# Token scaling ahead of the last weight maxima, and transfers of the token squares one step behind their data

## The chip, the cores and the metric

The kernel runs on 1 core of one Trainium2 chip. The metric is the device time of one execution in microseconds (us): the median of repeated runs of the whole kernel.

## The reference

A gated convolution over the sequence feeds a two-layer network:

```python
w = exp(weight_gen - max(weight_gen, -1)); w = w / (sum(w, -1) + 1e-09)      # 7 taps, 8 heads
out = einsum('bshk,bskhg->bshg', w, x_unf)      # x_unf: the 7 last rows of x, heads of 24
h = out.reshape(16384, 192) @ w_in              # w_in: 192 x 2048
g = maximum(0.01 * h, h)
return g @ w_out                                # w_out: 2048 x 192
```

All inputs and the output are float32.

## The kernel before, in words

The 16384 tokens are worked on in 32 chunks of 512 (`NCH`, `TOK`), and the 2048 hidden columns in 8 pairs of blocks of 128 (`NQ`). One call of `step(q)` (line 722) does pair i = q % 8 of chunk c = q // 8, so that step 8 is the first of chunk 1 and step 16 the first of chunk 2. In a step, `mm1` (line 495) forms the hidden values `hp` of two blocks in PSUM, ScalarE applies the leak and copies a float16 upper half `gh`, VectorE subtracts to get the lower half `gl` (`split_g`, line 525), and `mm2_pass` (line 548) multiplies halves of the step before with `wo` into the sums `po`. The second product is cut in two: `mm2_first` does two rows of the sums, then `tell` (line 570) puts an empty instruction on SyncE's queue that waits for its last matmul, and the first matmul of `mm2_second`, in the next step behind that step's `mm1`, waits for that empty instruction. SyncE's queue runs in order, so whatever stands ahead of a tell there holds it up. `hp` has four PSUM buffers, so that `mm1` of a step needs the buffers that `split_g` of the step but one before has read.

From chunk 1 on, both products run on pairs of float16 numbers: a token or weight is scaled by a power of two and split in an upper and a lower half. For the weights this needs the maxima over all blocks (`most`, line 186), joined by `weight_scales(0)`, `(1)` and `(2)` (line 212) across TensorE and VectorE into `scale`; `upper_half` (ScalarE) and `lower_half` (VectorE) then write `wi_h`, `wi_l` and `wo` block by block. Chunk 0 runs in float32 (`mm2_whole`, line 593, for its second product).

The tokens of chunk c + 1 go through a chain while chunk c is multiplied:

- GpSimd forms them by 13 operations of `conv_ops` (line 334), handed out by `feed`;
- `scale_tokens` (line 438): VectorE takes the maximum `xm`, computes the powers `xu` and `xd`, GpSimd multiplies (line 450);
- `split_h` (ScalarE, line 454) and `split_l` (GpSimd, line 463) make the halves; `split_h` also has VectorE compute `xr`, by which the sums are scaled back in `evacuate`;
- `squares` (line 467): four transposes of 32 x 32 blocks on VectorE;
- `put_squares` (line 478): SyncE sends them to DRAM (`far<-sq`), 384 KB;
- `get_squares` (line 485): SyncE waits for that and fetches them back in four transfers (`xx<-far`), 192 KB each, 32 partitions each. The first two feed the first half of the partitions of `mm1`, the last two the second half.

In `step`, `scale_tokens` comes in step i = `first`, the halves in `first + 1`, squares and `put_squares` in `first + 2`, `get_squares` in `first + 3`; `first` is 1, but 3 in chunk 1 and 2 in chunk 2 (`BEGIN`, line 43).

Everything before step 8 is ordered by hand in the string `START` (line 53): one letter for each action, in program order of all engines. The letters that matter here: `f` is `mm1` of the next pair of chunk 0 with its leaks, `e` the second product of one block of chunk 0, `m` the maximum of one weight block, `W` its rounding, `D` the division in the softmax of piece 1, `B` is `scale_tokens(1)`, `C` `split_h(1)`, `V` `split_l(1)`, `y` and `Y` the transposes of its two halves, `X` `put_squares(1)`, `R` `get_squares(1)`, `1 2 3` are the weight scales, `H` and `L` an upper and a lower half of a weight block, `q` one operation of chunk 2's convolution.

Of the kernel before, what the change touches and what calls it, by code (L numbers as in the profile page):

```python
# [8 lines left out]
F32 = mybir.dt.float32  # L9
F32R = mybir.dt.float32r  # L10
U32 = mybir.dt.uint32
I32 = mybir.dt.int32
F16 = mybir.dt.float16
AF = mybir.ActivationFunctionType
ALU = mybir.AluOpType
# [3 lines left out]
P = 128  # L19
# [20 lines left out]

HOLD = 2

BEGIN = {1: 3, 2: 2}

G0 = 20

# [9 lines left out]
    "rWrWmpf"  # L56
    "rWmrWmmKppeeeerWmprWmkppf"
    "rWmrWmMppf"
    "rWmrWmEpWmDpeeeef"
    "mmmmf"  # L60
    "B1e2e3CVyHLe"
    "HYLXe"
    "qRHLf"
    "qHLe"
    "qHLe"
)


# [1 line left out]
def conv_attention_moe_kernel(  # L70
# [8 lines left out]
    nc = tc.nc  # L79
# [8 lines left out]
    J = 4  # L88
# [16 lines left out]
    win = ctx.enter_context(tc.tile_pool(name="win", bufs=2))  # L105
# [77 lines left out]
    undo = const.tile([P, 1], F32, name="undo")  # L183
# [9 lines left out]
    def exponents(m, e):  # L193

        nc.vector.tensor_scalar(
            out=e, in0=m.bitcast(I32), scalar1=EXPONENT, scalar2=None, op0=ALU.bitwise_and
        )

    def powers(e, up, down):

        nc.vector.tensor_scalar(
            out=down, in0=e, scalar1=float(LEAST), scalar2=float(TOP * ONE),
            op0=ALU.max, op1=ALU.subtract,
        )
        nc.vector.tensor_scalar(  # L205
            out=up, in0=down, scalar1=-1.0, scalar2=float(254 * ONE),
            op0=ALU.mult, op1=ALU.add,
        )
# [56 lines left out]
    def load_weights(q, s=slice(0, R)):  # L265
        r0 = piece[q] * R
        if q not in wt:
            wt[q] = win.tile([P, R, HK], F32, tag="wt", name="wt")
        nc.sync.dma_start(out=wt[q][:, s, :], in_=w_rows[:, r0 + s.start:r0 + s.stop, :])

    def load_rows(q, parts=((0, PAD + R),)):
        r0 = piece[q] * R
        if q not in xt:
            xt[q] = xin.tile([P, PAD + R, D], F32, tag="xt", name="xt")
        if r0 > 0:
            for a, b in parts:
                nc.sync.dma_start(out=xt[q][:, a:b, :], in_=x_rows[:, r0 - PAD + a:r0 - PAD + b, :])
            return
        nc.sync.dma_start(out=xt[q][:, PAD:, :], in_=x_rows[:, 0:R, :])
        nc.gpsimd.memset(xt[q][0:1, 0:PAD, :], 0.0)  # L280
        for a, b in ((16, P), (1, 16)):
            nc.sync.dma_start(
                out=xt[q][a:b, 0:PAD, :], in_=x_rows[a - 1:b - 1, ROWS - PAD:ROWS, :]
            )
        for b in range(1, B):
            nc.gpsimd.memset(xt[q][b * PB:b * PB + 1, 0:PAD, :], 0.0)
# [9 lines left out]
    def softmax_max(q, s=ALL):  # L296
        if q not in mx:
            mx[q] = win.tile([P, R * H, 1], F32, tag="mx", name="mx")
            sm[q] = win.tile([P, R * H, 1], F32, tag="sm", name="sm")
        m = mx[q][:, s.start * H:s.stop * H, :]  # L300
        return nc.vector.tensor_reduce(out=m, in_=grouped(q, s), axis=AX.X, op=ALU.max).ins

    def softmax_sub(q, eng, s=ALL):
        eng.tensor_tensor(
            out=grouped(q, s), in0=grouped(q, s), in1=spread(mx[q], s), op=ALU.subtract
        )
# [86 lines left out]
    def new_xx(c):  # L393
        if c < WHOLE:
            xx[c] = xtp.tile([P, NK, 1, NB, P], F32, tag="xw", name="xw")
        else:
            xx[c] = xtp.tile([P, NK, 2, NB, P], F16, tag="xx", name="xx", bufs=2)
# [38 lines left out]
    split, sq, undo_of, downs = {}, {}, {}, {}  # L436

    def scale_tokens(c):

        m = win.tile([P, J, 2], F32, tag="xm", name="xm")[:, :, 0]  # L440
        e = win.tile([P, J, 2], I32, tag="xe", name="xe")[:, :, 0]
        up = win.tile([P, J, 2], I32, tag="xu", name="xu")[:, :, 0:1]
        down = win.tile([P, J, 2], I32, tag="xd", name="xd")[:, :, 0]
        nc.vector.tensor_reduce(  # L444
            out=m, in_=att[c], axis=AX.X, op=ALU.max, apply_absolute_value=True
        )
        exponents(m, e)
        powers(e, up[:, :, 0], down)
        downs[c] = down
        nc.gpsimd.tensor_tensor(  # L450
            out=att[c], in0=att[c], in1=up.bitcast(F32).to_broadcast([P, J, D]), op=ALU.mult
        )

    def split_h(c):
        split[c] = xtp.tile([P, 2, J, D], F16, tag="split", name="split")
        nc.scalar.copy(out=split[c][:, 0], in_=att[c])  # L456
        undo_of[c] = win.tile([P, J, 2], F32, tag="xr", name="xr", bufs=4)[:, :, 0]
        nc.vector.tensor_scalar(
            out=undo_of[c], in0=downs.pop(c).bitcast(F32), scalar1=undo, scalar2=None,
            op0=ALU.mult,  # L460
        )

    def split_l(c, eng):
        h, l = split[c][:, 0], split[c][:, 1]
# [2 lines left out]
    def squares(c, i):  # L467


        if i == 0:  # L470
            sq[c] = xtp.tile([P, 2, 2, NB, J, BK], F16, tag="sq", name="sq")
        src = split[c][:, i].rearrange("p j (b v d) -> p v b j d", v=2, d=BK)
        for v in range(2):
            nc.vector.transpose(out=sq[c][:, v, i], in_=src[:, v])  # L474
# [3 lines left out]
    def put_squares(c):  # L478

        away_of[c] = far.tile([P, 2, 2 * NB * TOK // NK], F16, tag="far", name="far")  # L480
        nc.sync.dma_start(
            out=away_of[c], in_=sq[c].rearrange("p v i b j t -> p v (i b j t)")
        )

    def get_squares(c):

        new_xx(c)
        dst = xx[c].rearrange("p k i b t -> p k (i b t)")
        src = away_of.pop(c).rearrange("(k d) v e -> v d k e", k=NK)
        for g in range(NK):  # L490
            nc.sync.dma_start(out=dst[g * BK:(g + 1) * BK], in_=src[g % 2])  # L491

    hp, g_h, g_l = {}, {}, {}

# [22 lines left out]
    def leak(n):  # L517
        return nc.scalar.activation(out=hp[n], in_=hp[n], func=AF.Prelu, alpha=0.01, scale=DOWN).ins  # L518
# [51 lines left out]
    def tell(ins):  # L570

        told = nc.sync.nop().ins  # L572
        tc.add_manual_dep(told, ins.name, after, reason="rows to leave")
        return told
# [12 lines left out]
    def mm2_second(ns, told):  # L587
        for i in range(HALF, J):
            mm2_pass(ns, i, told if i == HALF else None)
        for n in ns:  # L590
            del g_h[n], g_l[n]
# [85 lines left out]
    with tc.manual_schedule():  # L677
# [32 lines left out]
        def firsts(q):  # L710

            i = q % NQ
            return range(2 * q - (4 if i == 2 else 2), 2 * q if i != 1 and q < NP - 1 else 0)
# [8 lines left out]
        def step(q):  # L722

            c, i = divmod(q, NQ)
            if i == 0 and c in sm_q:
                load_weights(sm_q[c])
                load_rows(sm_q[c])
            if i == 1 and c in sm_q:
                softmax_max(sm_q[c])
                softmax_sub(sm_q[c], nc.gpsimd)  # L730
            begun, told = pending.pop() if pending else (None, None)
            mm1(q)
            leak(2 * q)
            if begun:
                mm2_second(begun, told)
                if begun[-1] % NF == NF - 1:
                    evacuate(begun[-1] // NF)
            split_g(2 * q)
            leak(2 * q + 1)
            split_g(2 * q + 1)  # L740
            if q == WHOLE * NQ:
                mm2_whole(range(2 * q - HOLD, 2 * q))
                evacuate_whole(c - 1)
            elif firsts(q):
                ns = firsts(q)
                pending.append((ns, tell(mm2_first(ns))))
            if c == WHOLE:
                for what in "HLHL" if i < 3 else "HL":
                    if done[what.lower()] < len(order):
                        prepare(what)  # L750
            if i == 0:
                feed(c + 1, 2 * K)
            if c + 1 < NCH:
                first = BEGIN.get(c, 1)
                if i == first:
                    scale_tokens(c + 1)
                if i == first + 1:
                    split_h(c + 1)
                    split_l(c + 1, nc.gpsimd)
                if i == first + 2:  # L760
                    squares(c + 1, 0)
                    squares(c + 1, 1)
                    put_squares(c + 1)
                if i == first + 3:
                    get_squares(c + 1)
                if i >= first:
                    feed(c + 2, 3)
            finish_softmax(c, i)
# [30 lines left out]
        for what in START.replace(" ", ""):  # L799
# [41 lines left out]
            elif what == "M":  # L841
                small[0] = spare()[:, 0:R * H].unsqueeze(2)
                nc.vector.tensor_reduce(
                    out=small[0], in_=grouped(1, ALL), axis=AX.X, op=ALU.max
                )
                nc.vector.tensor_tensor(
                    out=grouped(1, ALL), in0=grouped(1, ALL), in1=spread(small[0], ALL),
# [4 lines left out]
            elif what == "D":  # L852
# [6 lines left out]
                    out=grouped(1, ALL), in0=grouped(1, ALL), in1=spread(m, ALL), op=ALU.mult  # L859
# [60 lines left out]
```

## Time and profile before

| what | value |
|---|---|
| median of 3 runs | 1055.12 us (1053.99 to 1055.43) |
| the profiled execution's own time | 1056.53 us |
| its span | 1054.7 us |
| mean granted clock of TensorE | 0.993 |
| busy: TensorE, GpSimd, ScalarE, VectorE | 98%, 76%, 62%, 55% of the span |
| DMA | 83.06 MB, mean 79 GB/s |

All times in the trace count from the span's start. Busy shares are means over the span; the first hundred us, where chunk 0 in float32 gives way to chunks 1 and 2, look different from the rest, and the page's slices of 1/40 of the span show that: TensorE's granted clock is 0.8 to 0.9 of full speed in the third and fourth slice and full elsewhere after that. SyncE only issues transfers and empty instructions; its waits are shown as those of its queue (SPq).

### The profile page before, as it was taken

How to read it: one execution, taken by the hardware profiler on the slowest of the kernel's cores; microseconds unless marked ns; L12 is line 12 of the kernel's file. 1: busy time of each engine (PE TensorE's matmuls, PEld its weight loads, DVE VectorE, ACT ScalarE, POOL GpSimd, SP SyncE). 2: the span in 40 equal slices, each digit the busy share in tenths (PEclk: the TensorE clock that was granted, in tenths of full speed). 3: DMA queues.
4: the chain of work that ended last, by engine and by line, in shares of the span. 5: the costliest groups of instructions: out<-in, count | busy, mean ns of one | idle time of the engine just before them, and what ended most of it. 6: DMA issues, size and time to landing. Idle time of an engine off the chain costs nothing.

```text
span 1054.7 us, 30068 instructions
## 1 busy us (share of the span) xinstructions
PE 1035.8 (98%) x12700; PEld 669.0 (63%) x12700; DVE 581.1 (55%) x1056; ACT 655.8 (62%) x1238; POOL 804.5 (76%) x516
## 2 busy tenths in 40 slices
PE   9988999999999999999999999999999999999998
PEld 6654666666666666666666666566666666566665
DVE  7866555555565555555554555554555554555543
ACT  6555666666666665666665666665666665666664
POOL 6688787788777789777789777779777779977600
PEclk9988999999999999999999999999999999999999
DMA  9431121313213231231323222131230323220120
GB/s 232 130 121 46 54 101 46 123 46 95 90 43 97 62 122 47 61 106 34 122 61 109 61 60 94 47 123 46 68 117 31 108 61 107 62 61 32 47 62 16
DMA packets 42373, 83.06 MB, mean 79 GB/s; under 512 B 4479, under 2 KB 35839, under 8 KB 40446
## 3 DMA queue, kind: packets, MB, share of 16 engines
q1 hardware_dynamic: 42094, 80.95, 25.3%
q8 instruction: 99, 1.62, 0.7%
q14 instruction: 36, 0.29, 0.1%
q10 hardware_dynamic: 144, 0.20, 0.0%
HBM read 56.36 MB, written 24.77 MB: 77 GB/s over the span
## 4 chain that ended last, share of the span: by engine, by line
PE 85%; POOL 4%; DMA 4%; DVE 3%; ACT 2%; SPq 2%; issue 1%; DVEq 0%; POOLq 0%; ACTq 0%
PE hp L512 42%; PE po L558 42%; SPq L491 1%; DMA far<-sq 1%; DMA wi_raw<-in_moe_w_in_dram 1%; PE po L598 1%; POOL acc L349 1%; DMA xx<-far 1%; POOL split L465 1%; POOL tmp L345 1%; POOL acc L345 1%; POOL acc L450 1%; DVE xm L444 0%; ACT gh L532 0%; DVE sq L474 0%
## 5 line engine op out<-in xcount | busy, mean ns | idle before, releaser
L533 DVE TENSOR_TENSOR gl<-hp,gh 128x512 f16<-128x512 f32 x496 | 335.8, 686 | 345.4 <-ACT gh L532 343.7
L558 PE MATMUL po<-wo,gh 64*128 64x384 f16 x3968 | 510.5, 323 | 3.7 <-SPq L572 3.0
L558 PE MATMUL po<-wo,gl 64*128 64x192 f16 x3968 | 490.2, 243 | 0.4 <-DVE gl L533 0.4
L518 ACT ACTIVATE hp<-hp 128x512 f32<-128x512 f32 x496 | 292.4, 590 | 302.5 <-PE hp L512 302.5
L512 PE MATMUL hp<-xx,wi_h 64*128 64x512 f16 x2976 | 458.0, 378 | 6.4 <-DMA xx<-far 6.4
L349 POOL TENSOR_TENSOR acc<-acc,tmp 128x768 f32<-128x768 f32 x186 | 337.1, 1812 | 14.6
L558 PEld LDWEIGHTS <-gh 64*128 64x128 f16 x3968 | 220.8, 94 | 132.4 <-issue 12.2
L532 ACT CAST gh<-hp 128x512 f16<-128x512 f32 x496 | 290.7, 586 | 16.0 <-PE po L558 1.3
L512 PE MATMUL hp<-xx,wi_l 64*128 64x512 f16 x1488 | 297.5, 379 | 0.0
L345 POOL TENSOR_TENSOR tmp<-xt,wt 128x768 f32<-128x768 f32 x186 | 288.4, 1550 | 9.9
L512 PEld LDWEIGHTS <-wi_h 64*128 64x128 f16 x2976 | 159.0, 94 | 126.8 <-DMA xx<-far 5.9
L558 PEld LDWEIGHTS <-gl 64*128 64x128 f16 x3968 | 220.2, 94 | 21.7 <-DVE gl L533 0.8
L450 POOL TENSOR_TENSOR acc<-acc,xu 128x768 f32<-128x768 f32 x31 | 45.5, 1469 | 159.2 <-DVE xu L205 152.7
L512 PEld LDWEIGHTS <-wi_l 64*128 64x128 f16 x1488 | 83.7, 94 | 79.5 <-issue 1.7
L474 DVE STREAM_TRANSPOSE sq<-split 128x384 f16<-128x384 f16 x124 | 63.9, 554 | 48.9 <-POOL split L465 48.9
L641 DVE SCALAR_TENSOR_TENSOR ot<-po,xr,ot 128x192 f32<-128x192 f32 x124 | 43.3, 411 | 60.8 <-ACT ot L637 60.8
L456 ACT CAST split<-acc 128x768 f16<-128x768 f32 x31 | 25.8, 832 | 48.5 <-POOL acc L450 48.5
L465 POOL TENSOR_TENSOR split<-acc,split 128x768 f16<-128x768 f32 x31 | 51.4, 1659 | 1.9 <-ACT split L456 1.9
L345 POOL TENSOR_TENSOR acc<-xt,wt 128x768 f32<-128x768 f32 x31 | 47.8, 1542 | 0.1
L637 ACT ACTIVATE ot<-po,xr 128x192 f32<-128x192 f32 x124 | 42.1, 421 | 2.7 <-PE po L558 2.6
L444 DVE TENSOR_REDUCE xm<-acc 128x4 f32<-128x768 f32 x31 | 29.2, 943 | 0.0
L598 PEld LDWEIGHTS po<-bits,g 128*128 128x128 f32 x128 | 21.6, 198 | 3.2 <-issue 2.4
(80 smaller groups left out, 300.6 us busy)
## 6 DMA issues: line engine op xcount, KB each, us to landing
xx<-far SPq DMA_DIRECT2D x124, 192.0 KB, 3.8
xt<-in_x_dram SPq DMA_DIRECT2D x14, 1344.0 KB, 5.7
out_dram<-ot SPq DMA_DIRECT2D x63, 192.0 KB, 1.9
far<-sq SPq DMA_DIRECT2D x31, 384.0 KB, 2.3
wt<-in_weight_gen_dram SPq DMA_DIRECT2D x15, 224.0 KB, 2.6
wi_raw<-in_moe_w_in_dram SPq DMA_DIRECT2D x16, 192.0 KB, 5.4
wo_raw<-in_moe_w_out_dram SPq DMA_DIRECT2D x8, 384.0 KB, 4.9
xt<-in_x_dram SPq DMA_DIRECT2D x2, 384.0 KB, 5.0
```

The lines of the kernel that those rows point to most:

```text
L345: eng.tensor_tensor(out=out, in0=tap(c, k), in1=wk, op=ALU.mult)
L349: eng.tensor_tensor(out=acc, in0=acc, in1=out, op=ALU.add)
L450: nc.gpsimd.tensor_tensor(out=att[c], in0=att[c], in1=up.bitcast(F32).to_broadcast([P, J, D]), op=ALU.mult)
L465: eng.tensor_tensor(out=l, in0=att.pop(c), in1=h, op=ALU.subtract)
L474: nc.vector.transpose(out=sq[c][:, v, i], in_=src[:, v])
L512: nc.tensor.matmul(out=hp[2 * q + u], lhsT=w[u][s], rhs=r[s], start=(m == 0), stop=(m == len(passes) - 1),)
L518: return nc.scalar.activation(out=hp[n], in_=hp[n], func=AF.Prelu, alpha=0.01, scale=DOWN).ins
L532: nc.scalar.copy(out=h, in_=t)
L533: nc.vector.tensor_tensor(out=l, in0=t, in1=h, op=ALU.subtract)
L558: ins = nc.tensor.matmul(out=po[j // HALF][:, j % HALF, 0:d], lhsT=g[n][s, j * P:(j + 1) * P], rhs=wo[s, f, 0:d], start=(f == 0 and i < HA ...
L637: nc.scalar.activation(out=ot[:, j], in_=po[k][:, j, D:2 * D], func=AF.Copy, scale=rx[j])
L641: nc.vector.scalar_tensor_tensor(out=ot[:, j], in0=po[k][:, j, 0:D], scalar=rx[j], in1=ot[:, j], op0=ALU.mult, op1=ALU.add,)
```

## The change

Four things change. In `START`, `B` moves ahead of `D`; `C V y Y` come between the last four `m`, ahead of `1`; four `e` come ahead of `1`; `X` comes behind `1`, `R` behind `3`, and the last `f` behind only two more `e`. In `BEGIN`, chunk 1 scales the tokens of chunk 2 in its step 2 instead of 3, and chunk 2 those of chunk 3 in its step 1 instead of 2. In every chunk, `put_squares` comes one step later than `squares`, and `get_squares` one step after that. And `xr` is computed in `get_squares` instead of `split_h`, with three buffers for `xd`.

```diff
-BEGIN = {1: 3, 2: 2}
+BEGIN = {1: 2}
@@
     "rWmrWmMppf"
-    "rWmrWmEpWmDpeeeef"
-    "mmmmf"
-    "B1e2e3CVyHLe"
-    "HYLXe"
-    "qRHLf"
-    "qHLe"
-    "qHLe"
+    "rWmrWmEpWmBDpeeeef"
+    "CVymmYmmf"
+    "eeee1Xe2e3RHLHLHLf"
+    "qqHLHL"
@@ def scale_tokens(c):
-        down = win.tile([P, J, 2], I32, tag="xd", name="xd")[:, :, 0]
+        down = win.tile([P, J, 2], I32, tag="xd", name="xd", bufs=3)[:, :, 0]
@@ def split_h(c):
-        undo_of[c] = win.tile([P, J, 2], F32, tag="xr", name="xr", bufs=4)[:, :, 0]
-        nc.vector.tensor_scalar(
-            out=undo_of[c], in0=downs.pop(c).bitcast(F32), scalar1=undo, scalar2=None,
-            op0=ALU.mult,
-        )
@@ def get_squares(c):
             nc.sync.dma_start(out=dst[g * BK:(g + 1) * BK], in_=src[g % 2])
+        undo_of[c] = win.tile([P, J, 2], F32, tag="xr", name="xr", bufs=4)[:, :, 0]
+        nc.vector.tensor_scalar(
+            out=undo_of[c], in0=downs.pop(c).bitcast(F32), scalar1=undo, scalar2=None,
+            op0=ALU.mult,
+        )
@@ def step(q):
                 if i == first + 2:
                     squares(c + 1, 0)
                     squares(c + 1, 1)
+                if i == first + 3:
                     put_squares(c + 1)
-                if i == first + 3:
+                if i == first + 4:
                     get_squares(c + 1)
```

TensorE's instructions ahead of the first matmul of step 8, before (`ta` are transposes of chunk 0's tokens, `po_114<-bits,g` the second product of chunk 0, four instructions to a block, `xw` chunk 0's tokens):

```order
L512 MATMUL hp<-xw,bits 128x512 x12
L218 MATMUL spares<-ident,both 1x128 x2
L598 MATMUL po_114<-bits,g 128x192 x4
L226 MATMUL spares<-top,ones 128x2
L598 MATMUL po_114<-bits,g 128x192 x12
L512 MATMUL hp<-xw,bits 128x512 x6
L598 MATMUL po_114<-bits,g 128x192 x8
L512 LDWEIGHTS wi_h
```

and now:

```order
L509 MATMUL hp<-xw,bits 128x512 x12
L595 MATMUL po_114<-bits,g 128x192 x16
L215 MATMUL spares<-ident,both 1x128 x2
L595 MATMUL po_114<-bits,g 128x192 x4
L223 MATMUL spares<-top,ones 128x2
L595 MATMUL po_114<-bits,g 128x192 x4
L509 MATMUL hp<-xw,bits 128x512 x6
L509 LDWEIGHTS wi_h
```

Four blocks of the second product moved ahead of the transpose of the maxima `both`; the number of instructions is the same.

VectorE's instructions at the same place, before (`xm` to `xu` are the token maximum and its powers, the four on `spares` and `wt` the division, `sq` the transposes):

```order
L855 TENSOR_REDUCE spares<-wt 128x64
L856 TENSOR_SCALAR spares<-spares 128x64
L857 RECIPROCAL spares<-spares 128x64
L858 TENSOR_TENSOR wt<-wt,spares 128x448
L188 TENSOR_REDUCE most<-bits 128x1 x4
L444 TENSOR_REDUCE xm<-acc 128x4
...
L205 TENSOR_SCALAR xu<-xd 128x4
L215 TENSOR_REDUCE both<-most 128x2
...
L205 TENSOR_SCALAR scale<-back 128x2
...
L458 TENSOR_SCALAR xr<-xd,undo 128x4
L474 STREAM_TRANSPOSE sq<-split 128x384 x2
L250 SCALAR_TENSOR_TENSOR wi_l<-bits,scale,wi_h 128x384
L474 STREAM_TRANSPOSE sq<-split 128x384 x2
```

and now:

```order
L441 TENSOR_REDUCE xm<-acc 128x4
...
L202 TENSOR_SCALAR xu<-xd 128x4
L853 TENSOR_REDUCE spares<-wt 128x64
L854 TENSOR_SCALAR spares<-spares 128x64
L855 RECIPROCAL spares<-spares 128x64
L856 TENSOR_TENSOR wt<-wt,spares 128x448
L466 STREAM_TRANSPOSE sq<-split 128x384 x2
L185 TENSOR_REDUCE most<-bits 128x1 x2
L466 STREAM_TRANSPOSE sq<-split 128x384 x2
L185 TENSOR_REDUCE most<-bits 128x1 x2
L212 TENSOR_REDUCE both<-most 128x2
...
L485 TENSOR_SCALAR xr<-xd,undo 128x4
L247 SCALAR_TENSOR_TENSOR wi_l<-bits,scale,wi_h 128x384 x3
```

The tokens' maximum and transposes now stand ahead of `both`, on which the weight scales hang, and `xr` behind them.

VectorE's instructions in steps 10 to 14 of chunk 1 (`gl` are the lower halves of the hidden values, one pair to a step), before:

```order
L533 TENSOR_TENSOR gl<-hp,gh 128x512 x2
L250 SCALAR_TENSOR_TENSOR wo<-bits,scale,wo 128x2x192
L444 TENSOR_REDUCE xm<-acc 128x4
...
L533 TENSOR_TENSOR gl<-hp,gh 128x512 x2
L250 SCALAR_TENSOR_TENSOR wi_l<-bits,scale,wi_h 128x384
L458 TENSOR_SCALAR xr<-xd,undo 128x4
L533 TENSOR_TENSOR gl<-hp,gh 128x512 x2
L250 SCALAR_TENSOR_TENSOR wo<-bits,scale,wo 128x2x192
L474 STREAM_TRANSPOSE sq<-split 128x384 x4
```

and now:

```order
L441 TENSOR_REDUCE xm<-acc 128x4
...
L530 TENSOR_TENSOR gl<-hp,gh 128x512 x2
L247 SCALAR_TENSOR_TENSOR wo<-bits,scale,wo 128x2x192
L530 TENSOR_TENSOR gl<-hp,gh 128x512 x2
L247 SCALAR_TENSOR_TENSOR wi_l<-bits,scale,wi_h 128x384
L466 STREAM_TRANSPOSE sq<-split 128x384 x4
L530 TENSOR_TENSOR gl<-hp,gh 128x512 x2
L247 SCALAR_TENSOR_TENSOR wo<-bits,scale,wo 128x2x192
```

The maximum and the transposes stand one pair of `gl` earlier, the transposes now ahead of step 13's `gl` and `wo`. GpSimd's instructions and SyncE's transfers keep their order.

## Rows read from the trace of the kernel before

**Rows 1.** Timeline, TensorE, 39 to 70 us: start, us, form, idle before and releaser

```profile
46.60 0.38 PE L218 MATMUL spares<-ident,both 128*1 128x128 f32 x2 [1.77 <-DVE both L215]
...
55.39 2.87 PE L598 MATMUL po<-bits,g 128*128 128x192 f32 x16
59.81 0.37 PE L512 MATMUL hp<-xx,wi_h 64*128 64x512 f16 x1 [1.55 <-DMA xx<-far]
61.60 1.03 PE L512 MATMUL hp<-xx,wi_h 64*128 64x512 f16 x3 [1.42 <-DMA xx<-far]
...
69.33 0.61 PE L512 MATMUL hp<-xx,wi_h 64*128 64x512 f16 x4
```

**Rows 2.** Stretches of 2 us: busy time by engine, then granted clock, DMA share, GB/s

```profile
62.00:64.00 2.00, 2.00 (x12) 0.74 (x10) 0.00 (x0) 0.00 (x0) 1.92 (x2) 0.50 1.02 430
...
102.00:104.00 2.00, 2.00 (x12) 0.73 (x10) 0.00 (x0) 0.00 (x0) 1.92 (x2) 0.50 0.00 0
```

**Rows 3.** Chain of waits, 28 to 110 us: start, us, what

```profile
41.02 0.63 DVE spares L855
...
45.00 0.87 DVE xm L444
...
49.02 0.17 DVE scale L205
...
57.30 4.26 DMA xx<-far
```

**Rows 4.** Timeline, GpSimd, 34 to 70 us

```profile
46.62 1.47 POOL L450 TENSOR_TENSOR acc<-acc,xu 128x768 f32<-128x768 f32 x1 [6.54 <-DVE both L215]
```

**Rows 5.** Timeline, VectorE, 38 to 100 us

```profile
49.34 1.38 DVE L458 TENSOR_SCALAR xr<-xd,undo 128x4 f32<-128x4 f32 x1
...
53.49 3.02 DVE L250 SCALAR_TENSOR_TENSOR wi_l<-bits,scale,wi_h 128x384 f16<-128x384 f32 x2
...
58.25 2.15 DVE L250 SCALAR_TENSOR_TENSOR wi_l<-bits,scale,wi_h 128x384 f16<-128x384 f32 x1
...
81.41 0.95 DVE L444 TENSOR_REDUCE xm<-acc 128x4 f32<-128x768 f32 x1
...
91.75 1.04 DVE L474 STREAM_TRANSPOSE sq<-split 128x384 f16<-128x384 f16 x2 [0.60 <-POOL split L465]
```

**Rows 6.** Page, costliest groups: busy us, mean ns of one, idle before and releaser

```profile
L533 DVE TENSOR_TENSOR gl<-hp,gh 128x512 f16<-128x512 f32 x496 | 335.8, 686 | 345.4 <-ACT gh L532 343.7
```

**Rows 7.** Timeline, TensorE, at the end of chunk 1

```profile
95.56 0.34 PE L558 MATMUL po<-wo,gh 64*128 64x384 f16 x2 [0.70 <-DVE wo L250]
...
98.93 0.61 PE L512 MATMUL hp<-xx,wi_h 64*128 64x512 f16 x1 [2.21 <-DMA xx<-far]
100.73 1.03 PE L512 MATMUL hp<-xx,wi_h 64*128 64x512 f16 x3 [1.19 <-DMA xx<-far]
...
106.58 0.38 PE L512 MATMUL hp<-xx,wi_h 64*128 64x512 f16 x1
```

**Rows 8.** Waits of TensorE and of SyncE's queue: us in total, times, longest

```profile
PE po L558 <- SPq L572: 3.0, 5, 0.9
...
SPq L481 <- DVE sq L474: 160.9, 31, 18.3
```

**Rows 9.** Chain of waits: one `mm1` (876 to 935 us), and step 2's second product, chunks 5, 6, 31

```profile
884.96 1.94 PE hp L512 x18
...
210.07 2.94 PE po L558 x48
...
241.38 2.94 PE po L558 x48
...
1028.18 2.94 PE po L558 x48
```

**Rows 10.** Transfers `xx<-far`: issue in ns, min/median/max, and landing

```profile
L491 SPq DMA_DIRECT2D xx<-far x124: 319/430/1683, 56.0 to 1007.6; - x124
...
DMA to landing us min/median/max: 2.7/3.8/5.0
```

## The prediction

> **What bounds the kernel now.** The table of busy shares puts TensorE at 98% of the span, so the time is TensorE's work plus the little that it idles, plus what its clock loses. I read three views for that. The list of waits [rows 8] shows where TensorE waits: on the squares' transfers, and 5 times, 3.0 us together, on SyncE's queue. The timeline of TensorE [rows 1, 7] shows that the large waits lie in two places, just ahead of step 8 and ahead of step 16; there the reader is to look at the brackets. The stretches [rows 2] show what follows such a wait: TensorE is granted 0.50, that is 1.2 GHz in place of 2.4, and matmuls take twice as long for some 6 us. From chunk 2 on a chunk takes 31.31 us, as from 210.07 to 241.38 [rows 9], all matmul, and only the queue's waits add to it. The change touches all three losses. I write T(q) for the start of step q's first product.
>
> **Step 8's start.** Before, TensorE ends its chunk 0 products at 59.81 - 1.55 = 58.26 and begins step 8 in earnest at 61.60, when the second half of the squares has landed [rows 1]; ahead of that it idled 1.77 us for the maxima `both`. The change moves work without adding any instruction to TensorE. Four blocks of the second product, 2 x 2.87 = 5.7 us by the row of 16 records, now run from 46.60 - 1.77 = 44.83 to 50.6, where the idle 1.77 us was. They cover the maxima: `both` was ready at about 46.6, and four transposes, 2 x 1.04 us [rows 5], now stand ahead of it, which makes 48.7, with 1.9 us to spare for waits on GpSimd. So the 1.77 us go, and TensorE is ready for step 8 at 58.26 - 1.77 = 56.5.
>
> Are the squares there by then? The token maximum moves from 45.00 to 41.02, where the division began [rows 3], and its tokens are complete: GpSimd had idled 6.54 us before it scaled them at 46.62 [rows 4]. If all behind it keeps its distances, the last transfer lands at 57.30 + 4.26 - 3.98 = 57.6. Two things now stand behind the transposes that stood between: `xr`, 1.38 us, and a lower half of the weights, 1.5 us by the pair of 3.02 [rows 5]; instead two weight maxima stand there, shorter than either. That makes 55 at the other end. I take 56, nearer the second, since both pieces are gone for certain. Step 8 then starts at 56.5, 5.1 us earlier. The weight scales come later: the transposes of `both` at 50.6 in place of 46.6, so `scale` at 53.0 in place of 49.0. The first lower half is ready after `xr` and itself, 53.2 + 1.4 + 1.5 = 56.1, and is needed at the fifth matmul of step 8; covered, just.
>
> **The clock there.** From 61.60 to 69.33 TensorE ran one first product and two blocks of chunk 0 in 7.73 us at half clock [rows 1, 2]. At full clock they take 1.94 [rows 9] + 2.87 = 4.8 us. The fall came behind gaps of 1.55 and 1.42 us; the gap of 1.77 us earlier brought none, since the row at 55.39 is at full speed. With no gap ahead of step 8 I take full clock: T(9) = 56.5 + 4.8 = 61.3 in place of 69.33. **First term: 8.0 us** (bounds: 4 if the squares land at 57.6 and the clock still falls, 8.3 at best).
>
> **Chunk 1.** Now VectorE has less time for the weights' lower halves, because TensorE comes 5 to 8 us earlier and the scales 4 us later. From 53.2 it runs `xr` 1.4, five lower halves at 1.5 = 7.5, two `gl` at 0.69 [rows 6]: 63.5, which frees the PSUM buffers for step 10. TensorE gets there at 61.3 + 1.9 = 63.2, so 0.3 us late. Then VectorE runs a copy, two lower halves, a reduction and two `gl`: 3.0 + 1.4 + about 1.5 for copy and reduction = 69.4. The second product of step 10 has work on blocks 16 and 17 until about 66.4 and then waits for `gl` of block 18 at 68.7: T(11) is 2.4 us late in all. The bounds of this are 0 (lower halves that wait for nothing) and, at 2.15 us each [rows 5], about 4.6 us more.
>
> The token maximum `xm` of chunk 2 stood 81.41 - 69.33 = 12.1 us behind T(9). One step earlier is 31.31 / 8 = 3.9 us earlier, and VectorE is 2.4 late: 61.3 + 12.1 - 3.9 + 2.4 = 71.9. GpSimd's chain from there is unchanged: the transposes end 92.8 - 81.4 = 11.4 us behind `xm` [rows 5], at 83.3. They stand ahead of step 13's `gl` and `wo` now, which end 1.4 + 1.5 us later, at 86.2; step 14's second product wants them at about 85.6, so I add 0.6 us. In place of this wait the 0.70 us on `wo` at 95.56 [rows 7] goes. With five steps and these waits T(16) is due at 91.1. The fetch goes out when the tell of step 14 lets the queue go, at T(15) = 87.2; three issues of 0.43 [rows 10] and a landing of 4.26 make 5.6 us, 92.8. So TensorE still waits about 1.5 us for the second half there, where it waited 2.21 + 1.19 [rows 7]. If the clock holds, step 17 starts 3.8 us later (1.94 and as much of the second product), at 96.6, in place of 106.58: of those 10.0 us 8.0 are counted. **Second term: 2.0 us** (bounds: 3 lost to 5 gained).
>
> **The queue.** From 241.38 to 1028.18 25 chunks took 786.8 us; at 31.31 each 782.75 [rows 9]. The other 4.1 us are the 5 waits of 3.0 us and the refilling of the pipeline behind each. The cause is in the queue: the store waits for the transposes, 31 times, 160.9 us together [rows 8], the fetch waits for the store, and the step's tell stands behind both; one issue of 1.68 in place of 0.43 us [rows 10] then makes it late. Now the store stands behind the next step's tell, when the transposes are over or nearly so, and the fetch one more step on, when the store has landed. Nothing then blocks a tell. The fetch goes out two steps, 7.8 us, before its squares are needed and lands after 5.6, or 6.8 with a slow issue. **Third term: 4.1 us** (bounds 0 and 4.5).
>
> The Trainium skill (DMA: Bandwidth & Descriptors, Rules for kernel authors) says the opposite of this part: to overlap a transfer with compute, issue it early and wait late. By it the third term would be nothing at best and a loss where the cover ends. The rows decide otherwise, because the early issue itself made the queue wait.
>
> `xr` in its new place costs VectorE what it cost before; nobody waits for it until `evacuate`, a chunk later. The third buffer of `xd` costs nothing but space. Chunk 2 fetches in its step 5 before and after (2 + 3, 1 + 4), so its earlier scaling only gives the store more room, as in all later chunks.
>
> **The sum.** 8.0 + 2.0 + 4.1 = 14.1 us. The profiled execution took 1056.53 us, 1.4 above the median, and would take 1042.4; against the median of 1055.12 that is 1041.0.
>
> **The rivals.**
> 1. The clock falls again ahead of step 16. For it: a wait of 1.5 us remains, and others before it. Against it: 1.77 us did nothing before. From 100.73 to 106.58 took 5.85 us at half clock [rows 2, 7] against 3.8, so 2.1 us more: 1043.1. Chance 0.2.
> 2. VectorE becomes the bound of chunk 1: beside a busy GpSimd its operations stretch, as `xr`, on 4 values a partition, which took 1.38 us, and the lower half of 2.15 us [rows 5]. Seven lower halves stand ahead of block 18's `gl`; at 2.15 in place of 1.5 that is 4.6 us more, 1045.6. Against it: the pair of 3.02. The Trainium skill (SBUF — State Buffer, Who interferes with whom) gives the rule: a VectorE instruction with two SBUF inputs and a GpSimd one that reads SBUF share a port, and whichever comes second blocks until the other has ended. The row of `xr` agrees with such a wait. Chance 0.2.
> 3. The queue's waits stay, from a cause that I took for the transfers: 1045.1. Chance 0.07.
> 4. Slower: the fetch, a step later, no longer lands in time. It decides from 7.8 us behind the tell. Each us beyond costs some 30 us over 30 chunks; the first two terms pay for a third of a us, so from about 8.1 us on the kernel is slower, and at 8.8 it takes 1055.1 - 10 + 30 = 1075. Against it: a median landing of 3.8, 5.0 at most [rows 10]; even with the slowest issue that makes 1.68 + 2 x 0.43 + 5.0 = 7.5. Chance 0.03.
>
> That the change does not do what it says I rule out from the order of instructions, which shows the moves.
>
> **How the numbers follow.** My forecast, all three terms about as sized, has 0.5; the predicted time is its 1041.0, its own range 1038.5 to 1043. The range of 1038.5 to 1046.5 takes in rivals 1, 2 and 3. A measurement of this kernel tells 0.2%, 2.1 us, from no change. Only rival 4, and a failure of all terms at once, end above 1053.0: faster 0.94, same 0.03, slower 0.03.
>
> **What would show it.** Right: no idle of TensorE from 45 to 62 us and full clock throughout; `scale` near 53; step 9 near 61, step 17 near 97; the wait of TensorE on SyncE's queue gone, and a chunk of 31.3 us without exception. Wrong: half clock after 56 us, step 11 later than 72, or fetches that TensorE waits for in every chunk.

## The result and the profile after

| | before | changed |
|---|---|---|
| median of 4 runs, one chip | 1054.55 us (1053.38 to 1055.43) | 1043.43 us (1043.16 to 1044.05) |
| ratio with its 95% interval | 1 | 0.9896 (0.9879 to 0.9913) |
| profiled execution: own time, span | 1056.53, 1054.7 us | 1043.16, 1041.4 us |
| mean granted clock of TensorE | 0.993 | 0.997 |

The kernel is 11.1 us faster; 14.1 were forecast, with 1041.0 as the time and 1038.5 to 1046.5 as its range. The sign, the range and two of three terms held. Chunk 1 did not gain what it should. The profiled execution of before lost more to the clock than many others: its mean granted clock is 0.993, where the 29 executions measured beside the experiments have 0.992 to 0.997, ten of them 0.997, and one of the two falls of [rows 2] takes 3.4 us, 0.003 of the span; so what the clock is said to cost before holds for this execution.

Two profiled executions can be compared only from a common mark, because they don't reach chunk 0's last float32 products at the same time. TensorE's timeline has one group for those, in before:

```profile
39.41 5.42 PE L512 MATMUL hp<-xw,bits 64*128 64x512 f32 x24
```

and in the changed kernel:

```profile
37.70 5.42 PE L509 MATMUL hp<-xw,bits 64*128 64x512 f32 x24
```

TensorE's work ahead of this group is the same in both programs. Over all kernels here the group starts between 37.58 and 39.41 us, and one and the same kernel, profiled twice, had 39.14 and 37.70. So 1.7 us of the 13.3 by which the spans differ are scatter of the start. **Times called "from the mark" below count from this group**; "in before's time" adds 1.71 us to a time of the changed kernel.

| from the mark | before | changed | gained in this piece | forecast |
|---|---|---|---|---|
| T(9): 69.33, 59.45 | 29.92 | 21.75 | 8.2 | 8.0 |
| T(17): 106.58, 97.77 | 67.17 | 60.07 | -1.1 | 2.0 |
| end of span | 1015.3 | 1003.7 | 4.5 | 4.1 |

**Step 8.** TensorE's timeline of the changed kernel, where [rows 1] had three brackets:

```profile
48.36 0.38 PE L215 MATMUL spares<-ident,both 128*1 128x128 f32 x2
...
54.46 0.75 PE L509 MATMUL hp<-xx,wi_h 64*128 64x512 f16 x4
...
56.65 2.87 PE L595 MATMUL po<-bits,g 128*128 128x192 f32 x16
59.45 0.61 PE L509 MATMUL hp<-xx,wi_h 64*128 64x512 f16 x4
```

No row from the mark to step 10 has a bracket. Step 8's first product begins without a wait, and the two blocks behind it take 2.87 us, as the row at 55.39 in [rows 1], so the clock is full. VectorE's timeline has `both`:

```profile
47.20 0.17 DVE L212 TENSOR_REDUCE both<-most 128x2 f32<-128x16 f32 x1
```

It was ready at 47.37, 1.0 us before its transposes began at 48.36: the four blocks in front of them last longer than they need to.

**Chunk 1.** Here the brackets are. TensorE's timeline, the rows that waited over 0.25 us:

```profile
62.51 0.37 PE L509 MATMUL hp<-xx,wi_h 64*128 64x512 f16 x1 [0.94 <-DVE gl L530]
...
68.56 0.26 PE L555 MATMUL po<-wo,gl 64*128 64x192 f16 x2 [2.22 <-DVE gl L530]
...
87.24 0.34 PE L555 MATMUL po<-wo,gh 64*128 64x384 f16 x2 [0.28 <-DVE wo L247]
92.82 0.39 PE L509 MATMUL hp<-xx,wi_h 64*128 64x512 f16 x1 [0.53 <-DMA xx<-far]
94.08 0.60 PE L509 MATMUL hp<-xx,wi_h 64*128 64x512 f16 x3 [0.86 <-DMA xx<-far]
```

The two waits for `gl` are new. VectorE's timeline shows why:

```profile
51.97 1.55 DVE L485 TENSOR_SCALAR xr<-xd,undo 128x4 f32<-128x4 f32 x1
53.44 4.51 DVE L247 SCALAR_TENSOR_TENSOR wi_l<-bits,scale,wi_h 128x384 f16<-128x384 f32 x3
...
59.69 2.17 DVE L247 SCALAR_TENSOR_TENSOR wi_l<-bits,scale,wi_h 128x384 f16<-128x384 f32 x1
...
63.44 2.12 DVE L247 SCALAR_TENSOR_TENSOR wo<-bits,scale,wo 128x384 f16<-128x384 f32 x1
...
72.04 0.60 DVE L247 SCALAR_TENSOR_TENSOR wo<-bits,scale,wo 128x384 f16<-128x384 f32 x1
72.57 0.61 DVE L247 SCALAR_TENSOR_TENSOR wi_l<-bits,scale,wi_h 128x384 f16<-128x384 f32 x1
73.10 0.94 DVE L441 TENSOR_REDUCE xm<-acc 128x4 f32<-128x768 f32 x1
```

From 51.97 to 73.10 no row of VectorE has an idle bracket; it is the bound. A lower half takes 1.5 to 2.2 us until 67 us and 0.6 at 72. Between them GpSimd fell idle, as the bracket of its next row shows:

```profile
74.80 1.47 POOL L447 TENSOR_TENSOR acc<-acc,xu 128x768 f32<-128x768 f32 x1 [4.82 <-DVE xu L202]
```

GpSimd idled from 69.98 to 74.80: the same instruction of VectorE takes 0.6 us beside an idle GpSimd and, until 67 us, some three times as much beside a busy one. That GpSimd is the reason is tested below with `e8_one_tap`.

The stretches of 2 us show what the wait of 2.22 us did to the clock (column before the last two: granted clock):

```profile
68.00:70.00 2.00, 1.44 (x18) 0.81 (x20) 2.00 (x3) 0.36 (x1) 1.98 (x2) 0.93 0.00 0
70.00:72.00 2.00, 2.00 (x12) 0.77 (x10) 2.00 (x4) 0.00 (x0) 0.00 (x0) 0.50 0.00 0
72.00:74.00 2.00, 2.00 (x22) 0.96 (x18) 2.00 (x4) 0.58 (x1) 0.00 (x0) 0.72 0.00 0
```

The half clock of [rows 2] is back, but in step 11, where the prediction did not look for it, and not at step 8 or 16.

**The queue.** The chain of waits, step 2's second product of chunks 2, 3 and 31, in place of [rows 9]:

```profile
107.00 2.94 PE po L555 x48
...
138.31 2.94 PE po L555 x48
...
1014.84 2.94 PE po L555 x48
```

29 chunks in 907.84 us are 31.305 each: no excess is left. The list of waits, SyncE's queue, against [rows 8]:

```profile
SPq L473 <- DVE sq L466: 40.4, 30, 12.7
...
SPq L483 <- DMA far<-sq: 4.0, 4, 2.0
```

The store's waits fell from 160.9 to 40.4 us and the fetch waits 4 times in all; TensorE's row on SyncE's queue is gone. What remains of waits for fetched squares is this, and both of them stand at step 16 above:

```profile
PE hp L509 <- DMA xx<-far: 1.4, 2, 0.9
```

### The profile page after: what moved, and what is told of

It reads as the page before. It is cut to its first block, busy times and chain, and to the rows that moved or that the text cites. A ratio compares the mean times of both kernels' runs of the same rounds, so it can differ in the third digit from the quotient of the medians.

```text
span 1041.4 us, 30069 instructions
## 1 busy us (share of the span) xinstructions
PE 1029.7 (99%) x12700; PEld 679.7 (65%) x12700; DVE 574.8 (55%) x1056; ACT 655.9 (63%) x1238; POOL 804.4 (77%) x516
## 4 chain that ended last, share of the span: by engine, by line
PE 94%; DVE 3%; POOL 2%; DMA 1%; ACT 0%; issue 0%; SPq 0%; DVEq 0%; POOLq 0%
PE hp L509 47%; PE po L555 46%; PE po L595 2%; DVE wi_l L247 1%; DVE wo L247 1%; DVE gl L530 0%; DMA xx<-far 0%; POOL parts L374 0%; DMA wt<-in_weight_gen_dram 0%; POOL split L457 0%; POOL tmp L342 0%; POOL acc L346 0%; POOL parts L377 0%; SPq L483 0%; DVE xr L485 0%
## 5 line engine op out<-in xcount | busy, mean ns | idle before, releaser
L555 PEld LDWEIGHTS <-gh 64*128 64x128 f16 x3968 | 226.1, 94 | 119.3 <-issue 11.5
L555 PEld LDWEIGHTS <-gl 64*128 64x128 f16 x3968 | 225.2, 94 | 25.5 <-DVE gl L530 3.6
L509 PEld LDWEIGHTS <-wi_h 64*128 64x128 f16 x2976 | 162.5, 94 | 118.9 <-issue 3.3
```

The source lines that it names most:

```text
L509: nc.tensor.matmul(out=hp[2 * q + u], lhsT=w[u][s], rhs=r[s], start=(m == 0), stop=(m == len(passes) - 1),)
L555: ins = nc.tensor.matmul(out=po[j // HALF][:, j % HALF, 0:d], lhsT=g[n][s, j * P:(j + 1) * P], rhs=wo[s, f, 0:d], start=(f == 0 and i < HA ...
```

## The experiments

Each edit is made to the changed kernel. In every table line the interval is that of the ratio to before on the same chip.

| kernel | median us | ratio |
|---|---|---|
| `e1_old_start` | 1046.82 | 0.9939 (0.9922 to 0.9955) |
| `e2_no_step_later` | 1048.45 | 0.9951 (0.9936 to 0.9966) |
| `e3_fetch_alone_later` | 1044.36 | 0.9914 (0.9900 to 0.9929) |
| `e4_store_alone_later` | 1050.06 | 0.9965 (0.9953 to 0.9976) |
| `e5_chunk2_fetch_sooner` | 1043.19 | 0.9892 (0.9872 to 0.9912) |
| `e6_lower_halves_spread` | 1041.96 | 0.9882 (0.9863 to 0.9902) |
| `e7_both` | 1041.24 | 0.9876 (0.9856 to 0.9897) |
| `e8_one_tap` | 1039.33 | 0.9859 (0.9838 to 0.9879) |
| `after_again` (the changed kernel) | 1043.78 | 0.9898 (0.9879 to 0.9917) |
| `e9_blocks_back` | 1045.92 | 0.9916 (0.9897 to 0.9935) |
| `e11_three_blocks` | 1040.65 | 0.9865 (0.9847 to 0.9883) |
| `e7_again` (`e7_both` again) | 1041.35 | 0.9874 (0.9855 to 0.9892) |

Each four in the order of the table shared a chip; before took 1053.35, 1055.32 and 1054.53 us there.

### What the order at the start is worth

```diff
-    "rWmrWmEpWmBDpeeeef"
-    "CVymmYmmf"
-    "eeee1Xe2e3RHLHLHLf"
-    "qqHLHL"
+    "rWmrWmEpWmDpeeeef"
+    "mmmmf"
+    "B1e2e3CVyHLe"
+    "HYLXe"
+    "qRHLf"
+    "qHLe"
+    "qHLe"
```

> The change with the order of START put back to that of before; the queue's part and chunk 1's earlier scaling stay. Theory (VectorE bounds chunk 1, so that most of START's 8 us are given back there): the token maximum of chunk 2 comes one step earlier than before, the fetch goes out at the end of step 14, and step 17 starts about 5.4 us earlier than before, in place of 6.8 with the change; with the 4.5 us of the queue that is 1054.5 - 9.9 = 1044.6 us. Rival (START's part is worth its 8 us): 1043.4 + 8 = 1051.4 us.

It took 3.4 us more than the changed kernel, which was measured on another chip; by the ratios to before, 4.3 to 4.5. That lies between the two expectations, nearer the first. TensorE's timeline:

```profile
38.76 5.42 PE L512 MATMUL hp<-xw,bits 64*128 64x512 f32 x24
45.94 0.38 PE L218 MATMUL spares<-ident,both 128*1 128x128 f32 x2 [1.76 <-DVE both L215]
...
59.66 0.60 PE L512 MATMUL hp<-xx,wi_h 64*128 64x512 f16 x3 [1.73 <-DMA xx<-far]
...
61.70 2.87 PE L598 MATMUL po<-bits,g 128*128 128x192 f32 x16
64.50 0.61 PE L512 MATMUL hp<-xx,wi_h 64*128 64x512 f16 x4
...
90.50 0.50 PE L558 MATMUL po<-wo,gh 64*128 64x384 f16 x2 [3.57 <-DVE wo L250]
```

T(9) stands 64.50 - 38.76 = 25.74 from the mark. So of the 8.2 us of the first term the old order gives back only 4.0; the other 4.2 are there with the old order too. Before step 8 this kernel's instructions differ from before's by one thing alone: `xr` is out of `split_h` and stands behind the transposes. The store of the squares goes out 12.67 us from the mark (51.43 - 38.76) in place of 14.18 (53.59 - 39.41), 1.5 us sooner; one gap of 1.73 us is left of 1.55 and 1.42 [rows 1], and with it the clock holds: the two blocks at 61.70 take 2.87 us. By these two profiles the move of `xr` was worth about 1.3 us of idling and the 2.9 of the clock. It is not shown by an edit: `xr` was not put back alone, and the executions of before differ among themselves in what the clock costs. For the reading speaks that three of the four runs of `e1_old_start` have a mean granted clock of 0.998, above every one of before; but its earlier scaling in chunk 1 bears on that figure too.

Of the 4.0 us, 3.0 are left at T(17) (101.80 - 38.76 = 63.04 from the mark, against 60.07). VectorE holds up chunk 1 here too: the waits for `gl` are 0.52 us at most, but one for `wo` is 3.57 us, and behind it the clock falls to half (0.52 in the stretch from 90 to 92 us).

### Which transfer's delay frees the queue

Three edits for all chunks from 2 on; chunk 1 stays as changed. Neither one later:

```diff
-                if i == first + 3:
+                if i == first + (3 if c == 1 else 2):
                     put_squares(c + 1)
-                if i == first + 4:
+                if i == first + (4 if c == 1 else 3):
                     get_squares(c + 1)
```

> The change, but from chunk 2 on the store and the fetch each stand one step earlier again, as before the change; chunk 1 as in the change. Theory (the tells stood behind waiting transfers): TensorE waits on SyncE's queue some 5 times again, 3 us of idle time, and chunks of over 31.5 us return; 1043.4 + 4.5 = 1047.9 us. Rival (the waits had another cause): 1043.4 us.

The fetch alone later:

```diff
-                if i == first + 3:
+                if i == first + (3 if c == 1 else 2):
                     put_squares(c + 1)
```

> From chunk 2 on only the fetch stands one step later, the store in the step of its transposes. Theory (the fetch's wait for the store, with four issues behind it, is what made tells late; the store's wait for the transposes ends just in time): 1043.4 to 1044 us, TensorE's waits on the queue under 0.5 us. Rival (the store's wait, 160.9 us in total before, is the harmful one): 1047 to 1048 us.

The store alone later, the fetch right behind it:

```diff
-                if i == first + 4:
+                if i == first + (4 if c == 1 else 3):
                     get_squares(c + 1)
```

> From chunk 2 on the store stands one step later, and the fetch right behind it in the same step. Theory (the fetch's wait for the store harms): as without any delay, 1047 to 1048 us, with some 3 us of idle time of TensorE on the queue. Rival (the store's wait harms): 1043.4 us.

Measured: 1048.45, 1044.36 and 1050.06 us. From chunk 2 to chunk 31 the chain of waits gives 912.47, 907.90 and 913.25 us, against 907.84 in the changed kernel. TensorE's waits with neither later:

```profile
PE po L555 <- SPq L569: 3.2, 6, 0.8
```

and with the store alone later:

```profile
PE po L555 <- SPq L569: 3.4, 6, 1.8
```

With the fetch alone later no wait of a matmul on the queue is left, though the store still stands in the queue waiting for the transposes:

```profile
SPq L473 <- DVE sq L466: 152.1, 31, 12.7
```

So the forecast's sum for the queue was right and half of its cause was wrong. The store's long waits, 160.9 us before and 152.1 here, cost nothing, since no matmul waits behind them. The fetch costs: it waits for the store's landing (59.5 us in 30 times without the delay) and then puts four issues ahead of the tell. To delay the store alone is no better than to delay neither: the fetch still waits for its landing, 64.8 us in 30 times.

What makes a tell late is one long issue, as the prediction has it. With neither later, the four issues of a fetch take 1.75 to 2.03 us together in 23 chunks, and no matmul waits; in the other six one issue takes 1.17 to 1.73 us and the four 2.49 to 3.05, and those are the six waits. The chain of waits shows the first of them:

```profile
150.57 1.61 SPq L483
...
152.77 2.13 PE po L555 x32
```

The six waits are 3.2 of the 4.6 us by which chunks 2 to 31 are longer; where the rest goes is not shown.

Up to step 2 of chunk 2 these three, the changed kernel and its second measurement are one program. Chunk 2's row in the chain stands 69.30 to 69.69 us from the mark in these five profiles, so a tenth or two there means nothing. Behind the wait of 2.2 us in step 10 the clock fell in four of them. In `e2_no_step_later` it held at 1.00, and TensorE's timeline has instead:

```profile
69.28 0.26 PE L555 MATMUL po<-wo,gl 64*128 64x192 f16 x2 [2.22 <-DVE gl L530]
...
87.94 0.34 PE L555 MATMUL po<-wo,gh 64*128 64x384 f16 x2 [1.96 <-DVE wo L247]
```

TensorE came sooner to `wo` and waited 1.96 us for it in place of 0.28; behind that wait the clock fell in its turn (0.51 in the stretch from 90 to 92 us).

### Chunk 2's fetch

```diff
-                if i == first + 4:
+                if i == first + (3 if c == 1 else 4):
                     get_squares(c + 1)
```

> The change, but the fetch of chunk 2's squares stands in step 13 right behind the store, not behind the tell of step 14. In the change the store has landed at 86.8 us and the fetch went out at 88.55 us, when step 14's tell let the queue go. Theory (the queue holds up this fetch): step 16 starts in earnest up to 1.7 us earlier, 1041.7 us. Rival (something else ends last there, TensorE's own work or the wait for wo): 1043.4 us.

In the changed kernel SyncE's queue stored chunk 2's squares at 84.49 and fetched at 88.55, when step 14's tell had gone. One step sooner leaves one wait of 0.41 us in place of 0.53 and 0.86, and chunk 2's row in the chain stands 105.95 - 37.77 = 68.18 from the mark instead of 69.30. The trace gains 1.1 us; the medians of 1043.19 and 1043.43 don't resolve it.

### VectorE in chunk 1

The same weight halves in the same order, but one block in place of two in steps 8 and 9, two in steps 10 to 12, and those of step 10 behind the token maximum:

```diff
-            if c == WHOLE:
-                for what in "HLHL" if i < 3 else "HL":
+            if c == WHOLE and i != 2:
+                for what in "HLHL" if i in (3, 4) else "HL":
...
                 if i == first:
                     scale_tokens(c + 1)
+                    for what in "HLHL" if c == WHOLE else "":
+                        prepare(what)
```

> The change, but of the weight halves of chunk 1 one block instead of two in steps 8 and 9, two in steps 10 to 12, those of step 10 behind the token maximum. Theory (VectorE's lower halves, stretched beside GpSimd, bound chunk 1): the wait of 2.22 us in step 10 shrinks below 0.7, the clock does not fall, the token maximum of chunk 2 starts at about 70 in place of 73.1 us, and the whole takes 1040 to 1041 us. Rival (the work only moves behind the maximum and is late there for the second products): 1043 us or more.

It took 1041.96 us, 1.5 less, which the intervals don't resolve by themselves. TensorE's timeline:

```profile
67.02 0.26 PE L555 MATMUL po<-wo,gl 64*128 64x192 f16 x2 [0.40 <-DVE gl L530]
72.77 0.34 PE L555 MATMUL po<-wo,gh 64*128 64x384 f16 x2 [0.76 <-DVE wo L247]
85.85 0.34 PE L555 MATMUL po<-wo,gh 64*128 64x384 f16 x2 [1.20 <-DVE wo L247]
```

The wait of 2.22 us became 0.40, the clock stayed at 1.00 in every stretch from 38 to 112 us, and `xm` came at 70.65 in place of 73.10. New waits for `wo` took part of it back; step 2 of chunk 2 stands 68.02 from the mark, 1.3 sooner.

With chunk 2's fetch sooner as well:

> The two edits together: lower halves spread and chunk 2's fetch right behind its store. Theory: the gains add, 1038.5 to 1039.5 us. Rival (the fetch is no longer held up by the queue once VectorE is earlier): as with the spread alone, 1040 to 1041 us.

1041.24 us, and 1041.35 when it was run again. From the mark chunk 2's row stands at 66.98 to 67.10, 2.2 to 2.3 sooner than in the changed kernel, whose second measurement, on the chip of the second run of `e7_both`, gave 1043.78: the two edits together are worth 2.4 us there. That is less than the 4 to 5 us expected, but the gains do add: from the mark 1.1 and 1.3 us alone, 2.2 to 2.3 together. Each was smaller than its expectation.

> The change itself once more, beside the next three on one chip: about 1043.4 us, ratio 0.990.

> Lower halves spread and chunk 2's fetch right behind its store, once more, beside the change on one chip: 1041.2 us, some 2 us below the change.

Is it GpSimd that stretches VectorE? This kernel keeps it idle there:

```diff
+            if c == 2 and k < K - 1:
+                continue
```

> The change, but GpSimd forms chunk 2's tokens from one tap of seven, so it is idle while VectorE writes the lower halves; chunk 2's output leaves out six taps. Theory (the lower halves are slow because GpSimd is busy): they take 0.6 us each in place of 1.7, no wait in step 10, full clock, step 17 some 6 us earlier: 1036 to 1038 us. Rival (they are slow by themselves or wait for ScalarE): 1043 us.

It took 1039.33 us. GpSimd's and VectorE's timelines:

```profile
62.40 0.97 POOL L301 TENSOR_TENSOR wt<-wt,mx 128x448 f32<-128x448 f32 x1 [15.52 <-DVE mx L298]
```

```profile
51.03 0.23 DVE L487 TENSOR_SCALAR xr<-xd,undo 128x4 f32<-128x4 f32 x1
51.56 1.68 DVE L247 SCALAR_TENSOR_TENSOR wi_l<-bits,scale,wi_h 128x384 f16<-128x384 f32 x3 [0.30 <-ACT wi_h L241]
56.26 0.62 DVE L247 SCALAR_TENSOR_TENSOR wo<-bits,scale,wo 128x384 f16<-128x384 f32 x1 [3.02 <-ACT wo L241]
```

The columns are those of [rows 4] and [rows 5]. GpSimd idles 15.52 us, and in that time every lower half takes 0.6 us and `xr` 0.23 in place of 1.55; VectorE has brackets again, 3.02 us for ScalarE's upper half, and TensorE waits nowhere in steps 9 to 12. This shows why the lower halves are slow. The gain is 4.1 us by the medians, less than expected. The profiled execution, the slowest of the four with 1040.93 us, gains 2.2 us from the mark at chunk 2's row (104.76 - 37.62 = 67.14), of the 3.1 that the second term lacks, since TensorE meets its next waits: 1.89 us for `wo` at 83.03, 0.47 and 1.20 for the squares at 88.56 and 90.15, and there the clock falls:

```profile
90.00:92.00 2.00, 1.85 (x10) 0.68 (x12) 1.93 (x4) 0.00 (x0) 1.88 (x2) 0.61 0.00 0
92.00:94.00 2.00, 2.00 (x15) 0.96 (x13) 0.41 (x1) 0.45 (x1) 1.92 (x2) 0.54 0.00 0
```

In the two fastest of the four the mean granted clock is 1.000, so there it did not fall for that long.

### Where the four blocks stand

All four back behind the transposes of the maxima, to give VectorE the scales sooner:

```diff
-    "eeee1Xe2e3RHLHLHLf"
-    "qqHLHL"
+    "1Xe2e3eeRHLHLHLf"
+    "eqeqHLHL"
```

> The change, with the four blocks of chunk 0's second product put back behind the transposes of the maxima, the early tokens kept. TensorE then idles some 4 us ahead of the maxima, but the weight scales come 1.2 us earlier. Theory (VectorE bounds chunk 1 from the scales on): the 4 us are not lost; chunk 2 starts up to 1.2 us earlier, 1042 to 1043.5 us, as long as the clock does not fall. Rival (TensorE's idle time counts, as the first term of the prediction has it): 1047.5 us.

1045.92 us, 2.1 more than the changed kernel on that chip, between the two expectations: part of the idling comes back, part is absorbed. TensorE's timeline and stretches:

```profile
47.41 0.59 PE L215 MATMUL spares<-ident,both 128*1 128x128 f32 x2 [4.41 <-DVE both L212]
```

```profile
48.00:50.00 2.00, 2.00 (x7) 2.00 (x7) 0.41 (x1) 0.00 (x0) 1.86 (x2) 0.50 0.20 58
```

The idle time of 4.41 us halves the clock, and the block between the two transposes then takes 2.77 us instead of 1.47. So `scale` is ready at 51.62, no sooner than the 51.65 of the changed kernel: the idling buys nothing.

Three blocks ahead and one behind, with the edits of `e7_both`:

```diff
-    "eeee1Xe2e3RHLHLHLf"
+    "eee1Xe2e3eRHLHLHLf"
```

> Lower halves spread and chunk 2's fetch behind its store, and three instead of four blocks of the second product ahead of the transposes of the maxima, so that these run when the maxima are ready. Theory (VectorE from the scales on bounds): scales and chunk 2 about 1.2 us earlier than without the third edit, 1040 us. Rival (TensorE's own work bounds by now): as without it, 1041.2 us.

1040.65 us (1040.22 to 1041.04), the best of those that compute the whole output: 3.1 less than the changed kernel on that chip. Against `e7_again`, 0.7 less, which the medians don't resolve; from the mark, chunk 2's row stands at 104.45 - 38.63 = 65.82, 1.2 sooner. TensorE's timeline:

```profile
48.34 0.38 PE L215 MATMUL spares<-ident,both 128*1 128x128 f32 x2 [0.20 <-DVE both L212]
72.22 0.34 PE L555 MATMUL po<-wo,gh 64*128 64x384 f16 x2 [1.72 <-DVE wo L247]
85.30 0.34 PE L555 MATMUL po<-wo,gh 64*128 64x384 f16 x2 [1.20 <-DVE wo L247]
```

VectorE waits for the tokens now:

```profile
70.08 0.95 DVE L441 TENSOR_REDUCE xm<-acc 128x4 f32<-128x768 f32 x1 [1.60 <-POOL acc L346]
```

GpSimd's tokens of chunk 2 bound the token maximum, and the two waits for `wo` are what is left of VectorE's lateness. No run took these away.

## Why the prediction was right, and where it was wrong

1. **First term, right: 8.2 us by T(9) for 8.0.** In before's time, T(9) came at 61.2 (61.3 forecast) and `scale` at 53.4 (53.0). The squares were there before TensorE (the lower half that stood between the transposes had taken 1.02 us, not the 1.5 read from the pair, which changes nothing here), and the four blocks covered `both` with 1.0 us to spare (1.9 forecast): its transposes have no bracket, and with three blocks they wait 0.20 us. The order of `START` is not the whole of it: with the old order, `e1_old_start` still has 4.2 us of the 8.2, and by these two profiles that is the move of `xr` with the clock it saves; the order itself is worth 4.0.
2. **Second term, the step that failed: 2.0 us forecast, 1.1 lost.** Its sum took the lower halves at 1.5 us each. The five from `xr` to step 10's first product took 8.3 us, 1.67 each, and the two behind it 2.05 and 1.82; T(11) came 1.5 us later than forecast (71.2 in before's time for 69.7). The second fault is as large: `xm` was put at its old distance of 12.1 us behind T(9), less a step. That distance held idle time of VectorE; with none left, `xm` came as late as VectorE's queue was long, at 74.8 in place of 71.9. From there all went as worked out: the transposes end 11.4 us behind `xm` (84.46 - 73.10), the fetch goes out when step 14's tell lets it, TensorE waits 1.39 us for the squares (1.5 forecast), and T(17) is late by the same 2.9 us, 99.5 for 96.6.
3. **Third term, right: 4.5 us for 4.1**, with the cause in the fetch's wait and not in the store's. The size was read from the old trace as what it had above 31.31 us a chunk, so it did not hang on which of the two waits did the harm. The long issue behind a late tell was read rightly; that the refilling of the pipeline makes up what the waits leave is not shown.
4. **Rival 1** did not happen at step 16: with 0.53 and 0.86 us the clock held there. It happened in step 11, behind 2.22 us. Its price hardly shows: in the chain of waits the time from 51.97 to 74.66 is VectorE's, not TensorE's, and `e2_no_step_later`, where the clock held there, comes to chunk 2 no sooner (69.69 from the mark, against 69.30). That doesn't price the fall by itself, since there the clock fell later instead, behind 1.96 us.
5. **Rival 2** came in part: VectorE bound chunk 1 from 52 to 73 us, the longest lower halves took 2.17 and 2.12 us, near the 2.15 that it named, and its 4.6 us stand against 3.1 lost to the forecast. It deserved more than 0.2, since the changed order gave VectorE no idle time. The rule cited beside it, the Trainium skill (SBUF — State Buffer, Who interferes with whom), agrees with `e8_one_tap`: 0.6 us alone, 1.5 to 2.2 beside GpSimd. As cited it speaks of two inputs; `xr` has one tensor and a value for each partition, and that it waits too is shown by its 0.23 and 1.55 us alone.
6. **Rivals 3 and 4** are refuted: no matmul waits for the queue, and no fetch was waited for after chunk 2. Their landing of 2.6 to 5.4 us stayed inside the 7.8.
7. The rule of the Trainium skill (DMA: Bandwidth & Descriptors, Rules for kernel authors), issue early and wait late, would have had the third term at nothing or a loss. The runs here decide against it for this queue: `e2_no_step_later`, with the early issue, takes 5.0 us more (4.6 in the chain of waits).

Seen from the mark, the forecast missed by 14.1 - 11.6 = 2.5 us: the second term lacks 3.1, and the other two gave 0.6 more than theirs. Of the signs that the prediction named, no idle from 45 to 62 us (in before's time), `scale` near 53, step 9 near 61 and the even chunks came; full clock throughout and step 17 near 97 did not, and of the signs of being wrong one came, half clock after 56 us.

## What to carry to other kernels

On a queue that runs in order, ask of each waiting instruction what stands behind it: 160 us of waiting cost nothing, and 60 us of another wait in the same queue cost 4.5, because only the second kept a due instruction back. When a change fills the idle time of one engine, work out the queues of the engines that fed it anew; a distance read from the old trace holds their idle time, and that goes first. And mark a common start in two traces before subtracting them, and undo each part alone: by the profiles here, half of the largest term came with the move of one instruction on 4 values a partition, and only an edit that puts it back alone would settle that.

## What the runs showed of the hardware that was not expected

- One VectorE instruction with 128x384 values took 0.6 us beside an idle GpSimd and, from 53 to 67 us, 1.5 to 2.2 beside one that ran `tensor_tensor` back to back (later ones, where GpSimd runs too, 0.7 to 1.9); `xr`, on 128x4 values, took 0.23 and 1.55. The wait beside the other engine, not the work, set the price of this small instruction.
- Similar idle times of TensorE had different ends. The granted clock fell to half behind 1.55 and 1.42 us and behind 2.21 and 1.19 in before, behind one of 2.22 in the changed kernel, of 3.57 in `e1_old_start`, of 1.96 in `e2_no_step_later` and of 4.41 in `e9_blocks_back`, and in `e8_one_tap` behind 0.47 and 1.20. It held behind 1.76 and, later, 1.73 in `e1_old_start`, behind 1.20, 0.30 and 1.34 in `e6_lower_halves_spread`, and behind the same 2.22 in `e2_no_step_later`. The length of the gaps read here doesn't part the two groups: one and the same wait in one and the same program had both ends.
- Issuing one fetch takes SyncE 0.43 us as a rule, and up to 1.78 in the changed kernel too, with the queue's waits gone; what the long ones wait for stayed open.
